# Attention with a gated MLP on one core: transposes two tiles behind the scores and the values' products three

## Chip, core and metric

The kernel runs on one core of a Trainium2 chip. The metric is the device time of one execution in microseconds. A core has five engines that run side by side, each through its own queue in order: PE (TensorE, matmuls and transposes), DVE (VectorE), ACT (ScalarE), POOL (GpSimd) and SP, whose queue issues all DMAs of this kernel.

## What is computed

Banded causal attention with sinks for 4 batches of 8 heads, 768 positions and 64 columns a head; then, on its output, an MLP with a convolution of three taps in its gate.

```python
scores = q @ k.T / sqrt(64)                    # per batch and head
keep = (key < n_sink) | ((row - key >= 0) & (row - key < window))
a = softmax(where(keep, scores, -1e9))
x = concat_heads(a @ v)                        # 4 x 768 x 512
h = maximum(x @ w_in, 0)                       # 4 x 768 x 1024
c = cw[0]*prev_row(h) + cw[1]*h + cw[2]*next_row(h)
out = (h * sigmoid(c)) @ w_out                 # 4 x 768 x 512
```

n_sink is 4 and the window 128. The weights and the taps arrive as 64-bit numbers, everything else in 32 bits.

## The kernel before

**Tiles.** Heads go in pairs: four pairs a batch, 16 pairs in all, g = 0 to 15. A pair has six tiles of 128 rows, t = 0 to 5, in two halves of three. A tile needs the scores of its own 128 keys, of the 128 before, and of the sinks. `jobs` lists the (pair, half); batch 0 takes all first halves of its four pairs, then all second halves, later batches both halves of a pair in turn. `steps` has one entry for each of the 96 tiles.

**One tile** has three parts. `scores(g, t)` makes the scores of both heads in two PSUM buffers (sc). In batch 0 the mask is a matmul of PE (L521, before the product L337), DVE takes the row minimum (L523) and ACT the exponential (L532); later two products (L340, L341) are masked on DVE (L528, L529). DVE adds and inverts the sums (L534, L535), POOL normalises (L537). `transp(g, t)` transposes the normalised tile (pe, in batch 0 in roomH and roomL) on PE into pts (L553 in batch 0, L567 later), ACT copies it to pT (L555, L569), and POOL cuts it to the band (L571, L573). After a half's third tile the sinks' part is transposed too (L560, L581). `pv(g, t)` works at a half's third tile only: the products with the values (px: L598, L606; sinks' part L609), then xH and xL, the high and low part of x (L348, L349).

**The MLP** runs in units of 256 rows and 128 of the 1024 columns, 96 units: twelve products ph (L185), a gate on ACT, DVE and POOL (L192 to L203, of which L197, L198 and L200 are DVE's), and six products po (L212) two units later. A unit needs x of its rows, so the first eight start after batch 0's first halves, and each batch's units run beside the next batch's attention; those of the last batch run alone at the end.

**Weights.** Sixteen blocks of 128 x 512 and the taps are loaded, narrowed from 64 bits and split into a high and a low part by ACT (L113), DVE (L114, L115, L116, the cast L123) and POOL (L124), one block a step from step 2 to 18 (`WHEN`).

**Keys, queries, values.** `prep` transposes keys (trk, tk) and queries (trq, tq) ahead of their pair. From pair 4 on the keys stand in a tile kk whose halves are swapped by two DMAs (L301, L302). Two buffers serve kk; in batch 0 they are kks[0] and kks[1], and kks[1] also holds the sinks' values that L609 of batch 0 reads. `values(n)` loads the values of job n into one of two tiles vraw, by two DMAs; the tile was read by the products of job n - 2.

**What sets the order.** The loop hands out, in step i, the scores of step i in slot 0, the transposes of step i - D1 in slot 1 and the products of step i - D2 in slot 2, with pieces of MLP and of `prep` after each slot:

```python
for slot in range(SLOTS):
    if slot == 0 and i < NST:
        scores(g, t)
    if slot == 1 and 0 <= i - D1 < NST:
        transp(*steps[i - D1][1:])
    if slot == 2 and 0 <= i - D2 < NST:
        pv(*steps[i - D2][1:])
```

This order is a rank, not yet the order of an engine's queue: the program is built with `schedule_with_timeline_sim=True`, and in the compiled rows work stands ahead of work of a lower step where that was ready sooner. The functions that the diff touches:

Of the kernel before, what the change touches and what calls it, by code (L numbers as in the profile page):

```python
# [365 lines left out]
def load_v(c, g, slot, lo=0, hi=None):  # L366
    hi = hi or c.S // P
    load(c, g, "v", c.v_raw[slot][:, lo:hi], lo, hi)
    return c.v_raw[slot]
# [12 lines left out]
def sink_split(c, m, vsr, b):  # L382

    raw, hi, lo = (m.mp.tile([P, 512], d, tag="st", name=f"sink{n}{b}", bufs=3)[0:NS] for d, n in ((F32, "r"), (F32R, "h"), (F32R, "l")))
    c.nc.sync.dma_start(raw.rearrange("s (h d) -> s h d", d=D), c.v[b].rearrange("h s d -> s h d")[0:NS])
    c.nc.scalar.copy(hi, raw)
    c.nc.vector.tensor_tensor(out=lo, in0=raw, in1=f(hi), op=ALU.subtract)
    for u in range(3):
        for part, val in enumerate((hi, hi, lo)):
            for j in range(2):  # L390
                r = SR * part + 2 * NS * u + NS * j
                dst, src = (f(x).rearrange("s (g j d) -> s g j d", j=2, d=D)[:, :, j] for x in (vsr[r:r + NS, u], val))
                c.nc.sync.dma_start(dst, src)


def banded(c):
# [5 lines left out]
    NPAIR = c.H // 2  # L402
# [35 lines left out]
    def masks():  # L438
        nc.vector.tensor_scalar(before, R, 0.0, None, ALU.is_lt)
        nc.vector.tensor_tensor(out=m0, in0=own, in1=sk, op=ALU.max)  # L440
        nc.vector.tensor_copy(m1[:, 0:NS], tmp[:, 0:NS])
        nc.vector.tensor_copy(m2[:, 0:NS], sk[:, 0:NS])
        for mk in (m1, m2):
            nc.vector.tensor_tensor(out=mk[:, NS:KW], in0=own, in1=prv, op=ALU.max)
        for mk in (m0, m1, m2):
            nc.vector.tensor_scalar(mk, mk, -NEG, NEG, ALU.mult, ALU.add)
# [9 lines left out]
    def clear():  # L456
        w = vsr.shape[1] * vsr.shape[2] // 2
        for h in range(2):
            nc.sync.dma_start(f(vsr).rearrange("p u n -> p (u n)")[:, w * h:w * h + w], A.zeros[0:3 * SR, 0:w])
# [15 lines left out]
    jobs = [(g, half) for half in range(2) for g in range(NPAIR)]  # L475
# [13 lines left out]
    def fetch(upto=len(queue)):  # L489

        while free[0] and asked[0] < min(len(queue), upto):
            free[0] -= 1
            g, nm, half = queue[asked[0]]
            st[g].raw[nm, half] = load_half(c, g, nm, half, c.raw[asked[0] % RAWB])
            asked[0] += 1
# [89 lines left out]
    def pv(g, t):  # L585

        s = st[g]
        hp = g % NPAIR
        hf, u = divmod(t, 3)
        if u < 2:  # L590
            return
        px = ps.tile([P, 3, P], F32, tag="px", name=f"px{g}_{hf}").rearrange("p t k -> p (t k)")
        first = 3 * hf
        tiles = range(first + 2, max(0, first - 1) - 1, -1)
        if g < NPAIR:
            for n, (t1, w) in enumerate((t1, w) for t1 in range(t, first - 1, -1) for w in range(1 + (t1 > 0))):
                for j in range(2):
                    nc.tensor.matmul(px[D * j:D * j + D, P * (t1 - first):P * (t1 - first) + P], s.v[:, t1 - w, j, :],  # L598
                                     s.pT[t1][:, w, j, :], start=(n == 0), stop=False, skip_group_check=True)
            tiles = ()  # L600
        for kt in tiles:
            pT = s.pT.pop((kt, hf)).rearrange("p h a k -> p h (a k)")
            lo, hi = max(kt, first), min(kt + 1, first + 2)
            cols = slice(P * (lo - kt), P * (hi - kt) + P)
            for j in range(2):
                nc.tensor.matmul(px[D * j:D * j + D, P * (lo - first):P * (hi - first) + P], s.v[:, kt, j, :], pT[:, j, cols],  # L606
                                 start=(kt == tiles[0]), stop=False, skip_group_check=True)
        for w in range(1 - hf, 3):
            nc.tensor.matmul(px[:, P * w:P * w + P], (vsr if g >= NPAIR else c.vs)[:, w, P * hp:P * hp + P], s.sT, start=False, stop=(w == 2),  # L609
                             skip_group_check=True)  # L610
        A.xout(g, hf, px)

    def prep(n):

        g, half = jobs[n]
        if g >= NPAIR and half:
            return []
        if g >= PLAIN:
            return A.prep(g, st[g], ahead)
        out = []  # L620
        for h in (half, half + 1)[0:1 + g // NPAIR]:
            out += A.prep32(g, h, st[g], kks[g // 2][:, g % 2], "po" if g < NPAIR and h == 0 else "h", ahead)
        return out

    def values(n):
        g, half = jobs[n]
        if g < NPAIR:
            st[g].v = load_v(c, g, n % 2, *((2, T) if half else (0, 3)))
        elif half == 0:
            st[g].v = load_v(c, g, g % 2)  # L630

    def coming(n):

        last = 2 * NPAIR - 2
        if n < last:
            return [(n + 1, -0.4, 1.8)]
        if n == last:
            return [(n + 1, -0.4, 1.4), (n + 2, 1.4, 5.6)]
        return [(n + 2, -0.4 if n > last + 2 else 1.8, 5.1)] if n % 2 == 0 and n + 2 < len(jobs) else []
# [8 lines left out]
    steps = [(n, g, 3 * half + u) for n, (g, half) in enumerate(jobs) for u in range(3)]  # L648
    NST = len(steps)
    NSTB = NPAIR * T  # L650
    D1, D2 = 1, 2
    SLOTS = 3
    fill, todo, after = [], [], None
    rate = acc = 0.0
# [4 lines left out]
    for i in range(NST + D2):  # L659
        if i < NST:  # L660
            n, g, t = steps[i]
            if t % 3 == 0:
                for n1, lo, hi in coming(n):
                    new = prep(n1)
                    todo += [(i + lo + (hi - lo) * (k + 1) / len(new), x) for k, x in enumerate(new)]
            if g >= NPAIR or t % 3 == 2:
                fetch()
            if t == 0 and g and g % NPAIR == 0:
                after = i + 3 if g > NPAIR else i
            if i == after:  # L670
                sink_split(c, m, vsr, g // NPAIR)
            if n + 1 < len(jobs) and (t % 3 == 2 if n < 2 * NPAIR else t == 3):
                values(n + 1)
        if i == NSTB // 2:
            clear()
        if i == NSTB - 3:
            masks()
        m.need(min(sum(i >= w for w in WHEN), len(m.todo)))
# [7 lines that stand above are left out]
                if i - D2 + 1 in cuts:  # L686
                    while fill:
                        fill.pop(0)()
                    lo, hi, span = cuts[i - D2 + 1]
                    fill = m.pieces(lo, hi)  # L690
                    rate = len(fill) / (span - 0.5)
                    acc = 0.0
            acc += rate / SLOTS
            while acc >= 1.0 and fill:
                fill.pop(0)()
                acc -= 1.0
            while todo and i + (slot + 1) / SLOTS >= todo[0][0]:
                todo.pop(0)[1]()
# [73 lines left out]
def attention_gated_mlp(ctx: ExitStack, tc: tile.TileContext, q, k, v, n_sink, window, w_in, conv_w, w_out, out):  # L772
# [33 lines left out]
    with tc.If(fast == 1) as cmp:  # L806
        with ExitStack() as es:
            c.es = es
            banded(c)
# [32 lines left out]
```

## Time and profile before

| | us |
|---|---|
| three runs | 500.57, 503.0, 502.32; median 502.32 |
| the profiled execution | 501.29 |
| its span, first to last instruction | 499.6 |
| PE busy | 465.2 (93%) |
| DVE busy | 350.5 (70%) |
| ACT busy | 342.2 (69%) |
| POOL busy | 311.1 (62%) |

Busy times are sums over the whole span, which has stages with different limits. PE's busy time includes matmuls that overlap the one before, so a full PE shows 100% with spacing shorter than its rows' lengths. The views that matter are the busy time by stretch, the waits by engine, and single rows of the timeline (start, length, engine, line, operation, tile written <- tiles read).

### The profile page before, as it was taken

The page shows a single profiled execution, that of the slowest core. Times are in us where ns is not written, and L with a number is a line of the kernel's source. Part 1 is how long each engine was busy: PE and PEld are TensorE (multiplying, and loading weights), DVE is VectorE, ACT ScalarE, POOL GpSimd, SP SyncE. Part 2 cuts the span into 40 slices and gives each one's busy share as a digit, 9 for nine tenths or more (in the row PEclk, how much of TensorE's full clock was granted, in tenths as well). Part 3 has the DMA queues.
Part 4 walks back from the last instruction along what each step waited for, and adds up shares of the span by engine and source line. Part 5 has one row for each costly group of instructions (what it writes and reads, how often), then busy time and mean ns, then how long its engine had stood idle before and what let it go on. Part 6 is the DMA issues. An engine that isn't in the chain of part 4 may idle for free.

```text
span 499.6 us, 10664 instructions
## 1 busy us (share of the span) xinstructions
PE 465.2 (93%) x3301; PEld 398.3 (80%) x3301; DVE 350.5 (70%) x1140; ACT 342.2 (69%) x1072; POOL 311.1 (62%) x582
## 2 busy tenths in 40 slices
PE   1786889999999999999999999999999999999993
PEld 1564666888788788888888889898888888899982
DVE  5799999466778777877667687776676665655561
ACT  3877675777878877887776787786776754545541
POOL 3458768456759596786767767684764564444341
PEclk9999889999999999999999999999999999999999
DMA  6786833444341524415142231424021100101001
GB/s 156 202 232 176 216 94 87 93 110 113 108 113 33 141 47 97 94 27 141 47 107 52 61 109 33 100 61 98 2 75 33 43 2 0 45 1 43 22 23 50
DMA packets 87307, 41.04 MB, mean 82 GB/s; under 512 B 80160, under 2 KB 80184, under 8 KB 87240
## 3 DMA queue, kind: packets, MB, share of 16 engines
q1 hardware_dynamic: 87240, 40.25, 31.1%
q8 instruction: 29, 0.48, 0.4%
q14 instruction: 38, 0.31, 0.2%
HBM read 27.60 MB, written 6.29 MB: 68 GB/s over the span
## 4 chain that ended last, share of the span: by engine, by line
PE 77%; DVE 10%; ACT 4%; POOL 3%; DMA 2%; issue 2%; SPq 0%; POOLq 0%; DVEq 0%; ACTq 0%
PE ph L185 26%; PE po L212 25%; PE px L606 6%; PE sc L340 3%; PE sc L341 3%; PE pts L567 3%; PE tq L273 2%; PE px L609 2%; PE sc L337 2%; DVE stm L115 2%; PE px L598 1%; DVE stm L116 1%; PE tk L291 1%; POOL roomH L537 1%; PE pts L553 1%
## 5 line engine op out<-in xcount | busy, mean ns | idle before, releaser
L212 PE MATMUL po<-woH,g 128*128 128x512 f32 x384 | 142.9, 408 | 1.5 <-POOL g L202 1.5
L185 PE MATMUL ph<-xH,wiH 128*128 128x258 f32 (+1 forms) x384 | 112.2, 292 | 0.0
L185 PE MATMUL ph<-xH,wiL 128*128 128x258 f32 (+1 forms) x384 | 109.2, 284 | 0.0
L185 PE MATMUL ph<-xL,wiH 128*128 128x258 f32 (+1 forms) x384 | 109.1, 285 | 0.0
L202 POOL TENSOR_SCALAR g<-t 128x256 fp32r<-128x256 f32 x96 | 42.0, 438 | 68.6 <-DVE t L200 48.4
L197 DVE SCALAR_TENSOR_TENSOR t<-hb,cw,t 128x256 f32<-128x256 f32 x96 | 56.7, 591 | 32.8 <-ACT t L196 32.3
L212 PEld LDWEIGHTS po<-woH,g 128*128 128x128 f32 x384 | 69.3, 189 | 12.3 <-POOL g L202 2.5
L203 POOL TENSOR_TENSOR g<-t,g 128x256 fp32r<-128x256 f32 x96 | 75.2, 783 | 5.6
L537 POOL TENSOR_SCALAR pe<-pe,sm 128x132 f32<-128x132 f32 (+1 forms) x144 | 60.3, 430 | 27.8 <-DVE sm L535 18.8
L185 PEld LDWEIGHTS ph<-xH,wiH 128*128 128x128 f32 x384 | 73.0, 190 | 4.4 <-issue 1.3
L212 PE MATMUL po<-woL,g 128*128 128x512 f32 x192 | 76.4, 398 | 0.0
L185 PEld LDWEIGHTS ph<-xH,wiL 128*128 128x128 f32 x384 | 73.0, 190 | 2.2
L185 PEld LDWEIGHTS ph<-xL,wiH 128*128 128x128 f32 x384 | 72.9, 190 | 0.8
L532 ACT ACTIVATE pe<-pe,sm 128x132 f32<-128x132 f32 (+1 forms) x144 | 58.0, 406 | 14.0 <-DVE sm L529 13.1
L199 ACT ACTIVATE t<-t 128x256 f32<-128x256 f32 x96 | 40.2, 418 | 34.9 <-DVE t L198 34.4
L200 DVE SCALAR_TENSOR_TENSOR t<-t,hb 128x256 f32<-128x256 f32 x96 | 46.9, 489 | 18.0 <-ACT t L199 17.6
L198 DVE SCALAR_TENSOR_TENSOR t<-hb,cw,t 128x256 f32<-128x256 f32 x96 | 54.2, 564 | 4.5
L192 ACT ACTIVATE hb<-ph 128x258 f32<-128x258 f32 (+1 forms) x96 | 37.0, 386 | 27.5 <-PE ph L185 26.9
L196 ACT ACTIVATE t<-hb,cw 128x256 f32<-128x256 f32 x96 | 49.3, 514 | 7.3 <-POOL g L203 3.2
L528 DVE COPY_PREDICATED sc<-before,sc 128x128 f32<-128x128 int32 x120 | 33.6, 291 | 19.0 <-PE sc L341 17.7
L571 POOL TENSOR_SCALAR_AFFINE_SELECT pT<-pT 128x256 f32<-128x256 f32 x60 | 27.1, 451 | 31.1 <-ACT pT L569 28.3
L529 DVE CUSTOM_DVE_ANT_0 pe<-sc,m 128x132 f32<-128x132 f32 (+1 forms) x144 | 39.8, 289 | 8.6 <-PE sc L341 7.2
(147 smaller groups left out, 1030.3 us busy)
## 6 DMA issues: line engine op xcount, KB each, us to landing
raw<-in_q_dram SPq DMA_DIRECT2D x64, 96.0 KB
raw<-in_k_dram SPq DMA_DIRECT2D x64, 96.0 KB
out_dram<-stm SPq DMA_DIRECT2D x24, 256.0 KB
kk<-kk SPq DMA_DIRECT2D x24, 198.0 KB
vraw<-in_v_dram SPq DMA_DIRECT2D x24, 192.0 KB
wi_0r<-in_moe_w_in_dram SPq DMA_DIRECT2D x2, 512.0 KB
wi_1r<-in_moe_w_in_dram SPq DMA_DIRECT2D x2, 512.0 KB
wi_2r<-in_moe_w_in_dram SPq DMA_DIRECT2D x2, 512.0 KB
```

What stands on the lines that cost most here:

```text
L185: nc.tensor.matmul(u.h[:, 0:W], w[:, cc, ff * P:(ff + 1) * P], x[:, cc, t0:t1], start=(i == 0), stop=(i == len(prods) - 1))
L196: nc.scalar.mul(a, prev, cw[:, 0, ff:ff + 1])
L197: nc.vector.scalar_tensor_tensor(out=e, in0=this, scalar=cw[:, 1, ff:ff + 1], in1=a, op0=ALU.mult, op1=ALU.add)
L198: nc.vector.scalar_tensor_tensor(out=a, in0=nxt, scalar=cw[:, 2, ff:ff + 1], in1=e, op0=ALU.mult, op1=ALU.add)
L199: nc.scalar.activation(e, a, AF.Tanh)
L200: nc.vector.scalar_tensor_tensor(out=a, in0=e, scalar=1.0, in1=this, op0=ALU.add, op1=ALU.mult)
L202: nc.gpsimd.tensor_scalar(u.g[:, 0], a, 1.0, 1.0, ALU.mult, ALU.mult)
L203: nc.gpsimd.tensor_tensor(out=u.g[:, 1], in0=a, in1=f(u.g[:, 0]), op=ALU.subtract)
L212: nc.tensor.matmul(po[:, 0:c.DM], u.g[:, a, tt * P:(tt + 1) * P], w[:, ff, :], start=(ff == 0 and i == 0), stop=(ff == NFF - 1 and i == 2))
L529: nc.vector.tensor_tensor_reduce(out=pe[:, j, cols], in0=pc[:, P:SW][:, cols], in1=mk, op0=ALU.add, op1=ALU.min, scale=1.0, scalar=3.0e38, ...
L532: nc.scalar.activation(pe[:, j, cols], pcs[j][:, cols] if alone else pe[:, j, cols], AF.Exp, bias=sm[:, j:j + 1], scale=-1.0, accum_out=sm ...
L537: nc.gpsimd.tensor_scalar(pe[:, j, cols], pe[:, j, cols], sm[:, 8 + j:9 + j], 1.0, ALU.mult, ALU.mult)
```

## The change

D1 and D2 grow by one: a step hands out the transposes of the tile two steps back and the products of the tile three steps back; the loop runs one pass longer at its end, and the MLP's pieces, which are cut when a product is handed out, come one step later. The load of the next job's values moves from the head of the step, before its scores, to slot 2, behind that step's products.

```diff
-    D1, D2 = 1, 2
+    D1, D2 = 2, 3
     SLOTS = 3
...
             if i == after:
                 sink_split(c, m, vsr, g // NPAIR)
-            if n + 1 < len(jobs) and (t % 3 == 2 if n < 2 * NPAIR else t == 3):
-                values(n + 1)
...
                     rate = len(fill) / (span - 0.5)
                     acc = 0.0
+            if slot == 2 and i < NST and n + 1 < len(jobs) and (t % 3 == 2 if n < 2 * NPAIR else t == 3):
+                values(n + 1)
             acc += rate / SLOTS
```

Three places of the compiled order follow. In the names, sc_3_1 is a score buffer of tile 3, head 1; the last number is a running number.

First place: DVE at the cast of the last weight block (wo7r), in batch 0's second halves. Before:

```order
L523 TENSOR_REDUCE sm_170<-sc_5_1_997 128x1
L200 SCALAR_TENSOR_TENSOR t_943<-t_944,hb_114 128x256
L116 SCALAR_TENSOR_TENSOR stm_1029<-stm_1030,stm_1029 128x512
L523 TENSOR_REDUCE sm_171<-sc_3_0_1037 128x1
L534 TENSOR_REDUCE sm_170<-sm_170 128x2
L123 CAST woH<-stm_1029 128x512
L197 SCALAR_TENSOR_TENSOR t_1057<-hb_115,cw,t_1056 128x256
```

And now, with the same last cast of woH:

```order
L523 TENSOR_REDUCE sm_170<-sc_5_1_948 128x1
L197 SCALAR_TENSOR_TENSOR t_977<-hb_114,cw,t_976 128x256
L116 SCALAR_TENSOR_TENSOR stm_1010<-stm_1011,stm_1010 128x512
L349 TENSOR_TENSOR xL_117<-px_1_986,xH_116 128x384
L198 SCALAR_TENSOR_TENSOR t_976<-hb_114,cw,t_977 128x256
L534 TENSOR_REDUCE sm_170<-sm_170 128x2
L123 CAST woH<-stm_1010 128x512
L535 RECIPROCAL sm_170<-sm_170 128x2
L523 TENSOR_REDUCE sm_171<-sc_3_0_1018 128x1
L200 SCALAR_TENSOR_TENSOR t_976<-t_977,hb_114 128x256
```

The third unit's gate (L197, L198, L200) has moved later against the weights, its last row from before the cast to after it, and so has the next tile's first minimum (sc_3_0).

Second place: PE at the second score of the fourth tile of pair 2, which stands near that cast. Before:

```order
L212 MATMUL po_971<-woH,g_889 128x512
L212 MATMUL po_1010<-woH,g_889 128x512
L212 MATMUL po_1010<-woL,g_889 128x512
L212 MATMUL po_1010<-woH,g_889 128x512
L553 MATMUL pts<-ident,roomL 128x128 x4
L521 LDWEIGHTS identb
L521 MATMUL sc_3_1_1038<-apart_145,identb 128x260
L337 MATMUL sc_3_1_1038<-kks_165,X_901 128x260
L212 MATMUL po_971<-woH,g_950 128x512
```

And now:

```order
L315 MATMUL trq_1047<-ident,raw_69 128x128 x3
L185 MATMUL ph_1042<-xH_116,wiL 128x258
L185 MATMUL ph_1042<-xL_117,wiH 128x258
L185 MATMUL ph_1042<-xH_116,wiH 128x258
L185 MATMUL ph_1042<-xH_116,wiL 128x258
L553 MATMUL pts<-ident,roomL 128x128 x2
L521 LDWEIGHTS identb
L521 MATMUL sc_3_1_1019<-apart_145,identb 128x260
L337 MATMUL sc_3_1_1019<-kks_165,X_865 128x260
L553 MATMUL pts<-ident,roomL 128x128 x2
L185 MATMUL ph_1042<-xL_117,wiH 128x258
L212 MATMUL po_1006<-woH,g_920 128x512
```

The po products of the second unit (g_889 before, g_920 now) stood ahead of the score and now stand behind it; two of the four transposes too.

Third place: PE ahead of the first score of pair 5 (sc_0_0), which reads the second tile kk. Before:

```order
L185 MATMUL ph_1633<-xH_116,wiL 128x260
L185 MATMUL ph_1633<-xL_117,wiH 128x260
L609 MATMUL px_0_1717<-sT_0_1631,vsr 128x128 x2
L273 MATMUL tq_1642<-identr,nq_1638 128x128 x3
L567 MATMUL pts<-ident,pe_1_1600 128x128 x2
L273 MATMUL tq_1651<-identr,nq_1638 128x128 x3
L273 MATMUL tq_1712<-identr,nq_1708 128x128 x3
L340 MATMUL sc_0_0_1789<-kk_1569,X_1641 128x128
```

And now:

```order
L341 MATMUL sc_5_1_1686<-kk_1133,X_1308 128x260
L567 MATMUL pts<-ident,pe_1_1570 128x128 x2
L606 MATMUL px_0_1740<-pT_2_0_1654,vraw_71 64x128 x2
L606 MATMUL px_0_1740<-pT_1_0_1593,vraw_71 64x256 x2
L606 MATMUL px_0_1740<-pT_0_0_1519,vraw_71 64x256 x2
L273 MATMUL tq_1616<-identr,nq_1612 128x128 x3
L273 MATMUL tq_1626<-identr,nq_1612 128x128 x3
L567 MATMUL pts<-ident,pe_1_1570 128x128
L581 MATMUL tk_2_1658<-identr,sk_0_1659 72x128
L340 MATMUL sc_0_0_1760<-kk_1521,X_1615 128x128
```

The twelve ph of a unit, which stood between the products px of pair 4 and this score, have moved behind it. Counted back from this score to the transposes of the second half of the pair's keys (tk), there stood 12 ph and 9 tq among others; now there are one ph and 6 tq, beside the same px.

## Prediction before the run

> **What bounds the kernel now.** I read the stretches first, one row per stage: length, then busy time (and instructions) of PE, of PE's weight loads, of DVE, ACT and POOL, then clock, DMA share and GB/s.
>
> ```profile
> 12.00:25.00 13.00, 10.31 (x57) 7.92 (x58) 9.34 (x32) 10.62 (x36) 6.11 (x11) 1.00 0.77 207
> 25.00:84.00 59.00, 48.95 (x349) 37.87 (x348) 56.62 (x127) 41.11 (x121) 42.21 (x46) 0.94 0.62 170
> 84.00:100.00 16.00, 14.97 (x109) 11.76 (x108) 8.88 (x23) 11.66 (x34) 9.70 (x15) 1.00 0.33 74
> 100.00:200.00 100.00, 97.62 (x745) 84.02 (x743) 74.08 (x287) 78.84 (x272) 69.81 (x140) 1.00 0.39 95
> 200.00:425.00 225.00, 225.00 (x1632) 195.91 (x1631) 158.30 (x580) 162.79 (x532) 149.97 (x300) 1.00 0.24 60
> 425.00:499.60 74.60, 66.59 (x413) 59.31 (x411) 37.12 (x69) 33.09 (x77) 29.36 (x48) 0.99 0.09 31
> ```
>
> Two regimes. From 25 to 84 us VectorE is busy 56.62 of 59 us: it narrows and splits the weights beside the softmax, and only 2.4 us are left in it. From 84 us TensorE is the bound (225.00 of 225 between 200 and 425); the last 66 us are MLP alone. So a wait of PE counts only after 84 us, and a rearrangement before that counts only if it saves DVE time or leaves less PE work for later. PE's waits after 84 us, from the view of waits (total, times, longest):
>
> ```profile
> PE po L212 <- POOL g L202: 1.5, 2, 1.2
> PE pts L553 <- POOL roomL L537: 0.8, 1, 0.8
> PE sc L340 <- DVE sm L529: 0.7, 2, 0.5
> PE px L606 <- POOL pT L573: 0.5, 2, 0.3
> PE pts L567 <- POOL pe L537: 0.3, 1, 0.3
> PE sc L521 <- ACT roomH L532: 0.3, 1, 0.3
> PE tq L273 <- DVE kk L297: 0.2, 1, 0.2
> PE sc L521 <- ACT roomL L532: 0.2, 1, 0.2
> ```
>
> They sum to 4.5 us. The 1.2 of the first row is the last unit's gate near the end, which nothing here touches; 3.3 us remain. That is all a longer distance between a tile's scores and its transposes can win in the part where PE sets the time. Before 84 us PE waits much more, but under a busy DVE.
>
> **The change, part by part.** No instruction is added or removed; each loop step hands out the same scores with transposes and products of one step earlier. The rows of the compiled order show how little of that reaches the engines: the three places shown with the change differ by a fraction of a tile, since the order takes work when it is ready and the loop gives only its rank. Prices for PE work come from the chain of waits, in which saturated PE work has its true spacing (start, length, what):
>
> ```profile
> 367.11 1.46 PE ph L185 x12
> 369.04 0.33 PE tk L291 x3
> 370.95 0.12 PE sc L341
> 372.76 1.40 PE po L212 x6
> 374.16 0.22 PE pts L567 x2
> 374.70 1.23 PE px L606 x12
> 105.58 0.20 PE tq L273 x3
> ```
>
> (a) *DVE up to the last weight* (first place). The cast of the last weight block closes the DVE-bound stretch:
>
> ```profile
> 82.02 0.41 DVE L200 SCALAR_TENSOR_TENSOR t<-t,hb 128x256 f32<-128x256 f32 x1
> 82.95 0.42 DVE L523 TENSOR_REDUCE sm<-sc 128x1 f32<-128x260 f32 x1
> 83.35 0.41 DVE L123 CAST woH<-stm 128x512 fp32r<-128x512 f32 x1
> ```
>
> Counted from the first weight cast to this row, the order holds 148 DVE rows before and 146 now: the same weight work, 18 tiles' sums, five xL, three units' L197 and L198; one L523 and one L200 now come after it. That is 0.42 + 0.41 = **-0.8 us**.
>
> (b) *PE work left over.* At that cast PE stands, in both orders, near the second score of the fourth tile of pair 2 (82.75 us in the trace, the second place). Ahead of it stood 48 L185 and 12 L212; now 47 and 6. Six L212 cost 1.40, one L185 0.12. Two transposes of pe fewer (0.22 by the pts row) and three of q more (0.33, taken from the tk row) give back 0.1. So PE enters its saturated part with **+1.4 us** more to do: the lag delays the MLP's first products. Its bounds are 0 (PE, which had waits there, catches up) and one whole unit, 1.46 + 1.40 = 2.9.
>
> ```profile
> 82.75 0.27 PE L521 MATMUL sc<-apart,identb 128*128 128x260 bf16 x1
> ```
>
> (c) *Waits after 84 us.* Of the 3.3 us, none would go at worst and all at best. In the order the way from a tile's scores to its transposes, and between two scores in one buffer, has grown at more places than it has shrunk, though by far less than a tile. I take half, **-1.6 us**.
>
> (d) *The keys of pair 5.* Their tile is a buffer of batch 0, in which the sinks' values lie until the last L609 of that batch; the second half of the keys is transposed (tk), cast, and swapped between partition halves by two DMAs (L301, L302) before the pair's first score may run.
>
> ```profile
> 124.20 0.49 PE L291 MATMUL tk<-ident,raw 128*128 128x128 f32 x3
> 126.62 0.53 SPq L302 DMA_DIRECT2D kk<-kk  x1
> 130.63 0.30 PE L340 MATMUL sc<-kk,X 128*128 128x128 f32 x1
> 128.00:129.00 1.00, 1.00 (x11) 1.00 (x10) 0.96 (x6) 0.46 (x3) 0.54 (x2) 1.00 0.80 234
> 129.00:129.70 0.70, 0.69 (x7) 0.50 (x6) 0.51 (x2) 0.70 (x3) 0.70 (x2) 1.00 0.05 18
> ```
>
> The DMA share falls from 0.80 to 0.05 near 129 us, so tk to landing is about 4.8 us and tk to score was 6.4. The order now puts less PE work between them (third place): 3 tk (0.33), 1 ph (0.12), 4 score products (0.48), 3 pts (0.33), 12 px (1.23), 6 tq (0.40) and the sinks' transpose (0.1, one third of a tk row), 2.95 us together, against 4.8 before (11 ph more, the values' sinks, 3 tq, a pts). PE must then idle 4.8 - 2.95 = 1.9 us there; it idled 6.4 - 4.8 = 1.6 before. Were the keys slower by the whole 1.6 us of that slack, it would be 1.9 more; were they at once ready, 1.6 less. I take **+0.5**. Behind the waiting score on PE stands the MLP, and all of it is late by that much. On ACT the cast of the first half of these keys now stands ahead of the last xH of batch 0; both wait for the same L609, so xH is one cast later on an engine that is busy 78.84 of 100 us: 0.
>
> (e) *The loads of v* move from the head of a step to behind that step's product, and wait for the job before last, one step later. SP issues two of 0.97 us together; behind them in its queue now stands the load of wi_2r, which was ahead:
>
> ```profile
> 46.90 0.42 SPq L102 DMA_DIRECT2D wi_2r<-in_moe_w_in_dram  x1
> 47.38 0.97 SPq L357 DMA_DIRECT2D vraw<-in_v_dram  x2
> 57.82 0.85 DVE L115 SCALAR_TENSOR_TENSOR stm<-wi_2r,stm 128x512 int32<-128x512 int32 x1
> 18.79 4.39 DMA wi_2r<-in_moe_w_in_dram
> ```
>
> Such a block took 4.39 us to land when the chain waited for its twin, so there are 57.82 - 46.90 - 4.39 = 6.5 us of cover for a delay of one or two: **0**. If the cover were gone, DVE would wait in the stretch that it bounds, microsecond for microsecond. The v tiles themselves are read six steps later in batch 0 and eight later on: 0.
>
> (f) *The end.* One more pass of the loop; the last batch's MLP pieces still follow the last product on a full PE: 0.
>
> Sum: -0.8 + 1.4 - 1.6 + 0.5 + 0 = **-0.5 us** on an execution that took 501.29 us (span 499.6 and 1.7 around it), so 500.8. The three runs have their median 1.0 us higher, at 502.32 (500.57 to 503.0); on that footing **501.8 us**. About 0.5%, 2.5 us, is what a measurement of this kernel can tell from no change. My forecast is within it; by itself it has +-2 us, from the bounds of (b), (c) and (d).
>
> **Rivals.** *Faster:* the lag does what its name says, and every wait on a tile's chain goes: all 3.3 us after 84, DVE's 2.4 us of idle between 25 and 84, and no new wait at pair 5. 501.3 - 0.8 + 1.4 - 3.3 - 2.4 = 496.2, on the runs' footing **497.2 us**. For it: PE's waits for normalised tiles between 12 and 84 us, 5.5 us in two rows. Against it: DVE is busy 96% of the stretch from 25 to 84, and the order hardly moves. Chance 0.20.
>
> ```profile
> PE pts L553 <- POOL roomH L537: 3.5, 4, 1.5
> PE pts L553 <- POOL roomL L537: 2.0, 2, 1.7
> ```
>
> *Slower, by DVE and POOL in each other's way.* The same DVE instruction takes two very different times in the stretch that DVE bounds:
>
> ```profile
> 35.35 0.68 DVE L116 SCALAR_TENSOR_TENSOR stm<-stm,stm 128x512 int32<-128x512 int32 x1
> 46.17 1.62 DVE L116 SCALAR_TENSOR_TENSOR stm<-stm,stm 128x512 int32<-128x512 int32 x1
> L116 DVE SCALAR_TENSOR_TENSOR stm<-stm,stm 128x512 int32<-128x512 int32 (+1 forms) x15 | 13.7, 910 | 0.1
> ```
>
> The mean of 910 ns over 15 against 0.68 is 3.5 us, about four long ones at 0.94 us extra each. The order of weight work against softmax has changed, and POOL's normalisations and low halves fall beside other DVE rows. Four more long ones are +3.8: 501.8 + 3.8 = **505.6 us**; from three more it is slower than can be taken for noise. For it: nothing in the order avoids it; against it: as many could vanish. Chance 0.14.
>
> The Trainium skill, "SBUF — State Buffer", section "Who interferes with whom", has a rule for such pairs: a DVE instruction with two SBUF inputs and a GpSimd one that reads SBUF use one port pair under an exclusive lock, and the later one is blocked fully. The trace agrees so far as one and the same instruction takes 0.68 us at one place and 1.62 at another. By that rule which of the two starts first decides, which only the new trace shows; the sum could come out 3.5 us lower or higher by it, 498.3 to 505.3, and without it stays at 501.8.
>
> *The keys of pair 5 are late as a whole:* if the way from the last L609 of batch 0 to the first score of pair 5 (119.3 + 0.8 to 130.6, 10.5 us) has to be walked again, with 6.7 us of PE work in it now against 9.0 before (by the prices above: 18 ph, 3 tk, 3 tq, a pts and two of the sinks' products fewer, three po more), PE idles 3.8 instead of 1.5: +2.3 for +0.5, **503.6 us**. It decides when the work there is shorter than the way. Chance 0.08.
>
> ```profile
> 119.28 0.83 PE L609 MATMUL px<-sT,kks 96*128 96x128 f32 x6
> ```
>
> *The change does not do what it says,* since order follows readiness, is inside the forecast (502.3), whose chance is 0.58.
>
> **How the numbers follow.** The likeliest case gives 501.8. A little over half of the fast rival lies below 498.0 (0.11) and half of the port rival above 505.6 (0.07); that leaves out 0.18, so the range is 498.0 to 505.6. Faster by over 0.5%: the fast rival and 0.02 of the forecast's edge, 0.22. Slower: 0.14 and 0.04, 0.18. Within: 0.60.
>
> **What would show it.** In the new profile: (a) the last woH cast near 83 us, DVE near 56 of 59 us before it; (b) twelve instead of eighteen L212 before the first score of the next tile; (c) the pts and sc rows of PE's waits after 84 us halved, the rest the same; (d) a wait of a microsecond or two ahead of the first L340 of pair 5; (e) no wait of DVE or ACT on a weight load that was not there before. A cast later than 86 us, with L115 and L116 longer, means the port rival; a PE wait of over 2 us at pair 5 the keys; a cast before 81 us the fast one. What would make it all wrong is a wait that the order cannot show, in a queue that I priced at nothing.

## Result and profile after the change

| | before | after |
|---|---|---|
| median of the runs side by side, us | 501.77 (4 runs) | 508.99 (4 runs) |
| ratio, 95% interval | | 1.0143 (1.0113 to 1.0173) |
| the profiled execution, us | 501.29 | 508.26 |
| its span, us | 499.6 | 506.3 |

The kernel became 1.4% slower, 3.4 us above the upper end of the predicted range. The stretches of the changed kernel, with the columns of the prediction's first view:

```profile
12.00:25.00 13.00, 10.20 (x54) 7.55 (x55) 9.01 (x31) 10.23 (x34) 6.01 (x10) 1.00 0.76 201
25.00:84.00 59.00, 48.23 (x348) 37.45 (x349) 55.89 (x122) 39.86 (x116) 41.84 (x45) 0.94 0.61 171
84.00:100.00 16.00, 13.48 (x86) 10.89 (x86) 10.09 (x27) 12.26 (x36) 11.18 (x16) 0.89 0.35 78
100.00:200.00 100.00, 98.38 (x748) 84.71 (x748) 70.09 (x282) 78.38 (x265) 65.86 (x136) 1.00 0.38 93
200.00:425.00 225.00, 225.00 (x1600) 193.51 (x1599) 157.14 (x581) 163.20 (x535) 151.63 (x301) 1.00 0.24 61
425.00:506.30 81.30, 73.82 (x466) 65.39 (x464) 40.89 (x76) 36.07 (x83) 32.53 (x51) 0.99 0.08 28
```

The telling row is the fifth, and in it not the busy time but the count. PE is busy 225.00 of 225 us in both kernels, at the same clock, and does 1600 matmuls instead of 1632. At 225 / 1632 = 0.138 us each the missing 32 are 4.4 us. The other loss is ahead of 200 us: 24 matmuls fewer (1236 for 1260), 3.3 us by the same price, 23 of them between 84 and 100. A few records can be missing, so these are sizes, not accounts; they sum to 7.7 where the profiled executions differ by 7.0. Between 84 and 100 us the granted clock was also lower, 0.89 against 1.00, which these counts include.

PE's waits after 84 us in the changed kernel (total, times, longest):

```profile
PE sc L521 <- ACT roomH L532: 2.5, 1, 2.5
PE po L212 <- POOL g L202: 1.2, 1, 1.2
PE sc L340 <- DMA kk<-kk: 0.7, 1, 0.7
PE pts L567 <- POOL pe L537: 0.5, 1, 0.5
PE px L606 <- POOL pT L573: 0.2, 1, 0.2
PE ph L185 <- DVE kk L297: 0.2, 1, 0.2
```

Most of the small waits on a tile's chain went, as hoped for in (c). One of 2.5 us came. The timeline shows it on PE, and on ACT the queue ahead of the exponential that it waits for:

```profile
84.52 0.40 PE L212 MATMUL po<-woH,g 128*128 128x512 f32 x1
87.44 0.27 PE L521 MATMUL sc<-apart,identb 128*128 128x260 bf16 x1 [2.52 <-ACT roomH L532]
```

```profile
84.53 0.42 ACT L199 ACTIVATE t<-t 128x256 f32<-128x256 f32 x1 [2.37 <-DVE t L198]
85.38 0.62 ACT L386 CAST sinkh<-sinkr 4x512 fp32r<-4x512 f32 x1 [0.44 <-DMA sinkr<-in_v_dram]
85.91 1.03 ACT L252 ACTIVATE X<-trq,headscale 128x384 f32<-128x384 f32 x2
86.84 0.45 ACT L532 ACTIVATE roomH<-sc,sm 128x260 f32<-128x260 f32 x1
```

ACT stood idle for 2.37 us at a gate's step, then for 0.44 at the sinks' cast, with the exponential behind both.

The loss after 200 us is in no row of waits. It is seen where one half's products L606 stand in PE's order. Pair 9's second half in the compiled order of the changed kernel, with what stands between its pieces (running numbers left out):

```
L606 MATMUL px9_1<-pT9_5_1,vraw 64x128 x2
L291 MATMUL tk110<-ident,raw 128x128 x3
L606 MATMUL px9_1<-pT9_4_1,vraw 64x256 x2
L606 MATMUL px9_1<-pT9_3_1,vraw 64x256
L212 MATMUL po320<-woH,g32 128x512
L212 MATMUL po320<-woL,g32 128x512
L606 MATMUL px9_1<-pT9_3_1,vraw 64x256
L606 MATMUL px9_1<-pT9_2_1,vraw 64x128
L212 MATMUL po320<-woH,g32 128x512
...
L606 MATMUL px9_1<-pT9_2_1,vraw 64x128
```

Each operand pT serves two products, one for each head of the pair; a product fills 64 of the array's columns (128*64 in the trace), and is two matmuls there. This half is broken three times, twice between the two heads of a pair. From batch 1 on there are 24 halves; their products stood in 29 pieces before (5 breaks, 4 inside a pair of heads) and stand in 40 now (16 breaks, 11 inside). The changed kernel's timeline at this half, PE and then its weight loads:

```profile
258.04 0.44 PE L606 MATMUL px<-pT,vraw 128*64 128x128 f32 x4
258.41 0.55 PE L291 MATMUL tk<-ident,raw 128*128 128x128 f32 x3
258.88 1.08 PE L606 MATMUL px<-pT,vraw 128*64 128x256 f32 x6
259.89 0.50 PE L212 MATMUL po<-woH,g 128*128 128x512 f32 x1
260.23 0.39 PE L212 MATMUL po<-woL,g 128*128 128x512 f32 x1
260.55 0.65 PE L606 MATMUL px<-pT,vraw 128*64 128x256 f32 x4
261.12 0.73 PE L212 MATMUL po<-woH,g 128*128 128x512 f32 x2
...
262.25 0.43 PE L606 MATMUL px<-pT,vraw 128*64 128x128 f32 x2
262.61 0.39 PE L340 MATMUL sc<-kk,X 128*128 128x260 f32 x1
```

```profile
258.41 0.31 PEld L291 LDWEIGHTS tk<-ident,raw 128*128 128x128 f32 x3 [0.17 <-ACT t L199]
258.88 0.62 PEld L606 LDWEIGHTS px<-pT,vraw 128*64 128x64 f32 x6 [0.17 <-issue]
259.89 0.19 PEld L212 LDWEIGHTS po<-woH,g 128*128 128x128 f32 x1 [0.38 <-POOL g L202]
...
260.55 0.20 PEld L606 LDWEIGHTS px<-pT,vraw 128*64 128x64 f32 x4 [0.36 <-issue]
261.12 0.30 PEld L212 LDWEIGHTS po<-woH,g 128*128 128x128 f32 x2 [0.38 <-issue]
...
262.25 0.19 PEld L606 LDWEIGHTS px<-pT,vraw 128*64 128x64 f32 x2 [0.36 <-issue]
262.61 0.19 PEld L340 LDWEIGHTS sc<-kk,X 128*128 128x128 f32 x1 [0.17 <-issue]
```

From the start of a piece to the start of what follows it: 0.37 + 1.01 + 0.57 + 0.36 = 2.31 us for sixteen matmuls. At seven of the eight crossings between these and full-array matmuls the weight load, which otherwise runs beside the matmul ahead, stands still: for 0.36 to 0.38 us where work of 256 or 512 columns stood ahead, for 0.17 us behind work of 128 columns alone. At the first crossing (258.04) no idle time is listed.

### The profile page after: what moved, and what is told of

The parts are those of the page before. It is cut to its first block, busy times and chain, and to the rows that moved or that the text cites. A ratio compares the mean times of both kernels' runs of the same rounds, so it can differ in the third digit from the quotient of the medians.

```text
span 506.3 us, 10673 instructions
## 1 busy us (share of the span) xinstructions
PE 470.9 (93%) x3301; PEld 401.1 (79%) x3301; DVE 349.3 (69%) x1140; ACT 344.1 (68%) x1072; POOL 313.0 (62%) x582
## 4 chain that ended last, share of the span: by engine, by line
PE 82%; DVE 9%; DMA 3%; ACT 2%; issue 1%; POOL 1%; SPq 0%; POOLq 0%; ACTq 0%; DVEq 0%
PE ph L185 27%; PE po L212 26%; PE px L606 7%; PE sc L340 4%; PE sc L341 3%; PE pts L567 3%; PE tq L273 2%; DVE stm L115 2%; DVE stm L116 2%; PE px L609 2%; PE sc L337 2%; PE tk L291 2%; PE px L598 2%; PE pts L553 1%; DVE sm L523 1%
## 5 line engine op out<-in xcount | busy, mean ns | idle before, releaser
L197 DVE SCALAR_TENSOR_TENSOR t<-hb,cw,t 128x256 f32<-128x256 f32 x96 | 56.9, 592 | 34.9 <-ACT t L196 34.0
L537 POOL TENSOR_SCALAR pe<-pe,sm 128x132 f32<-128x132 f32 (+1 forms) x144 | 62.6, 447 | 25.8 <-DVE sm L535 18.4
L199 ACT ACTIVATE t<-t 128x256 f32<-128x256 f32 x96 | 40.1, 418 | 38.9 <-DVE t L198 38.4
L200 DVE SCALAR_TENSOR_TENSOR t<-t,hb 128x256 f32<-128x256 f32 x96 | 46.5, 485 | 17.4 <-ACT t L199 16.7
L198 DVE SCALAR_TENSOR_TENSOR t<-hb,cw,t 128x256 f32<-128x256 f32 x96 | 53.0, 552 | 5.3 <-DVE t L197 0.5
L340 PE MATMUL sc<-kk,X 128*128 128x260 f32 (+1 forms) x144 | 44.5, 316 | 0.8 <-DMA kk<-kk 0.7
```

The lines of the kernel that those rows point to most:

```text
L197: nc.vector.scalar_tensor_tensor(out=e, in0=this, scalar=cw[:, 1, ff:ff + 1], in1=a, op0=ALU.mult, op1=ALU.add)
L198: nc.vector.scalar_tensor_tensor(out=a, in0=nxt, scalar=cw[:, 2, ff:ff + 1], in1=e, op0=ALU.mult, op1=ALU.add)
L199: nc.scalar.activation(e, a, AF.Tanh)
L200: nc.vector.scalar_tensor_tensor(out=a, in0=e, scalar=1.0, in1=this, op0=ALU.add, op1=ALU.mult)
L340: self.nc.tensor.matmul(pc, X[:, j, u, :], kk[:, j, lo:hi], start=True, stop=False)
L537: nc.gpsimd.tensor_scalar(pe[:, j, cols], pe[:, j, cols], sm[:, 8 + j:9 + j], 1.0, ALU.mult, ALU.mult)
```

## The experiments

Two of these kernels (e7, e8) only set D1 and D2 and the place of the load of v. In the others PE, DVE, ACT, POOL and SP keep a compiled order, with the named instructions moved by hand. For that a function at the end of the kernel ties each instruction to the one ahead of it on its engine, by edges that order but do not wait:

```python
for a, b in zip(names, names[1:]):      # one row of names for each engine
    c.tc.add_manual_dep(made[b], a, info, reason="order")   # info: NoSync
```

Holding an order in this way costs nothing that shows: e2, which holds the changed kernel's order with two instructions moved, took 508.96 us, the changed kernel 508.99. In e1 to e4 two lines of imports push all line numbers up by two (L608 there is L606). All were timed in five rounds beside the kernel before; ratios are to it.

### Mending the breaks: e1 and e4

Edit, on PE alone; here at the half shown above (e4 the same on the kernel before):

```diff
-L606 MATMUL px9_1<-pT9_5_1,vraw 64x128 x2
 L291 MATMUL tk110<-ident,raw 128x128 x3
-L606 MATMUL px9_1<-pT9_4_1,vraw 64x256 x2
-L606 MATMUL px9_1<-pT9_3_1,vraw 64x256
...
+L606 MATMUL px9_1<-pT9_5_1,vraw 64x128 x2
+L606 MATMUL px9_1<-pT9_4_1,vraw 64x256 x2
+L606 MATMUL px9_1<-pT9_3_1,vraw 64x256 x2
+L606 MATMUL px9_1<-pT9_2_1,vraw 64x128 x2
```

> The changed kernel, its order held on every engine by order-only edges, with one thing moved: on PE the products L606 of one half, which stand in 40 pieces for 24 halves (29 before the change), stand in 24, each half where its last piece was; nothing is left out. Theory A, that PE pays about 0.3 us for each break of such a group (in the trace 0.20 us from L606 to what follows and 0.09 us back): 16 breaks fewer, 508.3 - 4.6 = 503.7 us. Theory B, that the loss is the wait of 2.5 us at 84 us and the half clock behind it, and that the slow growth after 180 us is something else: 508.3 us. Theory C, that pieces fill holes in which PE would wait: slower, by up to the 16 holes of 0.1 to 0.3 us, 510 to 513 us.

> The kernel before the change, order held, the products L606 of a half kept together: 24 pieces instead of 29. Theory A: 5 breaks by 0.29 us, 501.3 - 1.5 = 499.8 us. Theory B: 501.3 us. Theory C: 501.8 to 503 us.

Measured: e1 502.00 us, 1.0006 (0.9992 to 1.0020), 7.0 us less than the change; e4 498.63 us, 0.9935 (0.9916 to 0.9954), 2.7 us less than its session's 501.28. Theory A holds in sign; its price of 0.29 us a break was too low: 7.0 / 16 = 0.44 and 2.7 / 5 = 0.53. The same stretch as above, in e1 and in e4, and a whole half of sixteen matmuls in e1:

```profile
200.00:425.00 225.00, 224.13 (x1645) 197.47 (x1645) 160.03 (x583) 163.67 (x536) 154.60 (x303) 1.00 0.24 60
```

```profile
200.00:425.00 225.00, 225.00 (x1653) 197.88 (x1652) 158.77 (x583) 165.02 (x538) 151.92 (x304) 1.00 0.24 61
```

```profile
312.11 1.52 PE L608 MATMUL px<-pT,vraw 128*64 128x128 f32 x16
313.56 0.39 PE L342 MATMUL sc<-kk,X 128*128 128x260 f32 x1
```

In this stretch e1 does 45 matmuls more than the changed kernel, and e4 does 21 more than the kernel before. Whole, a half takes 1.45 us where it took 2.31 in four pieces.

### Breaking them on purpose: e5 and e6

Edit, on PE, in each of e4's 24 halves: the instruction ahead of the half goes behind its second pair (e5) or behind the first product of the second pair (e6):

```diff
-L567 MATMUL pts<-ident,pe10_0 128x128
 L606 MATMUL px9_1<-pT9_5_1,vraw 64x128 x2
 L606 MATMUL px9_1<-pT9_4_1,vraw 64x256 x2
+L567 MATMUL pts<-ident,pe10_0 128x128
 L606 MATMUL px9_1<-pT9_3_1,vraw 64x256 x2
```

> The kernel of e4 (before the change, the products L606 of a half kept together), with each of the 24 halves broken once, behind its second pair of heads: the one PE instruction that stood ahead of the half stands in the break. Nothing is left out. In the trace the two heads' products of 256 columns start 7 ns apart and the next pair 0.21 us later, and a half costs 0.10 us more where it goes over to another line and 0.09 us where it is come back to. By that a break between pairs costs 0.2 us: 498.6 + 24 x 0.2 = 503.4 us. If every break costs the same, whatever it parts (0.41 us, the 6.6 us of e1 by 16): 508.5 us. If breaks are not the cause, and e1 and e4 are faster for another reason that comes with the order: 498.6 us.

> As e5, but each half broken once inside a pair, behind the first head's product of the second pair. If the price is that the two heads' products no longer run side by side: 0.2 us as in e5, and 0.21 us for the product that now runs alone, 498.6 + 24 x 0.41 = 508.4 us. If every break costs the same: the same as e5. If breaks are not the cause: 498.6 us.

Measured: e5 508.25 us, 1.0130 (1.0108 to 1.0151); e6 516.74 us, 1.0298 (1.0274 to 1.0322). Against e4 that is 9.6 / 24 = **0.40 us** for a break between pairs and 18.1 / 24 = **0.75 us** inside one. Both prices are about twice the expected ones, and they differ, so it is not any break alike. The timeline of PE at one and the same half of six products (pairs of 128, 256 and 256 columns), with a query's transpose L273 in the break, in e5 and then in e6:

```profile
304.51 0.87 PE L606 MATMUL px<-pT,vraw 128*64 128x128 f32 x8
305.31 0.28 PE L273 MATMUL tq<-identr,nq 128*128 128x128 f32 x1
305.52 0.65 PE L606 MATMUL px<-pT,vraw 128*64 128x256 f32 x4
306.11 0.44 PE L273 MATMUL tq<-identr,nq 128*128 128x128 f32 x3
```

```profile
307.52 0.86 PE L606 MATMUL px<-pT,vraw 128*64 128x128 f32 x6
308.32 0.28 PE L273 MATMUL tq<-identr,nq 128*128 128x128 f32 x1
308.53 1.08 PE L606 MATMUL px<-pT,vraw 128*64 128x256 f32 x6
309.54 0.28 PE L273 MATMUL tq<-identr,nq 128*128 128x128 f32 x1
```

From start to next start, the first piece takes 0.80 us in both, though in e6 one of its products has gone; the second piece takes 0.59 us in e5 and 1.01 with that product in it. So a lone product takes the time of a pair. When they are not parted, the second head's product runs beside the first in the other 64 columns: 1.01 - 0.59 = 0.42 us is the price of parting them, 0.35 by the runs (0.75 - 0.40). My expectation had counted a product as one matmul, where the trace has two, and so at half its price.

### One lag at a time: e7 to e10

Edit of e7: `D1, D2 = 2, 2`, the load of v at its old place. Edit of e8: `D1, D2 = 1, 3`, the load moved as in the change. e9 and e10 are e7 and e8 with their breaks mended as in e1. (There is no run with the load of v moved alone. With D1 and D2 as before, that move leaves the compiled order of PE, DVE, ACT and POOL as it was; in SP's queue one load of v falls behind two stores of the output.)

> The transposes trail by two tiles, the products by two as before, the loads of v at their old place; the order is what comes of it. On PE the products L606 have 18 breaks, 11 of them inside a pair (before 5 and 4, after 16 and 11). Counting 0.2 us for a break and 0.21 more inside a pair, 5.9 us against 1.8 before: 501.3 + 4.1 = 505.4 us, and up to 2.5 us more if the losses ahead of 150 us come with the transposes: 507.9 us. If the longer lag of the products is the cause: 501.3 us.

> The products trail by three tiles, with the loads of v moved as in the change, the transposes by one as before. On PE the products L606 have 14 breaks, 8 of them inside a pair: by the same count 4.5 us against 1.8 before, 501.3 + 2.7 = 504.0 us, and up to 2.5 us more if the losses ahead of 150 us come with the products: 506.5 us. If the transposes' lag is the cause: 501.3 us.

> The kernel of e7 (only the transposes trail by two), order held, its 18 breaks of the products L606 mended on PE; nothing is left out. If the breaks are the whole of its loss, at the 0.44 us (e1) to 0.53 us (e4) that a mended break gave: 507.5 - 18 x 0.44 to 0.53 = 498.0 to 499.6 us, level with e4. If the longer lag of the transposes costs something by itself, the rest of it stays: above 500.5 us.

> The kernel of e8 (only the products trail by three), order held, its 14 breaks mended. By the same price: 502.1 - 14 x 0.44 to 0.53 = 494.7 to 495.9 us. By its own trace, in which PE's progress falls behind that of the kernel before by only 2.1 us after 180 us, so that its breaks are cheap ones: 502.1 - 2.1 - 2.9 (what e4 gained there) = 497.1 us. If a longer lag of the products gains nothing and e8's trace misleads: 498.6 us, level with e4.

| transposes, products trail by | as compiled | breaks (inside a pair) | breaks mended |
|---|---|---|---|
| 1, 2 (before) | 501.77 | 5 (4) | e4 498.63, 0.9935 (0.9916 to 0.9954) |
| 2, 2 | e7 507.53, 1.0121 (1.0099 to 1.0144) | 18 (11) | e9 497.80, 0.9934 (0.9910 to 0.9957) |
| 1, 3 | e8 502.06, 1.0012 (0.9997 to 1.0026) | 14 (8) | e10 495.68, 0.9885 (0.9866 to 0.9904) |
| 2, 3 (the change) | 508.99, 1.0143 (1.0113 to 1.0173) | 16 (11) | e1 502.00, 1.0006 (0.9992 to 1.0020) |

e7, e9 and e10 came within 0.2 us of their expectations; e8 came 1.9 us below the 504.0 counted from its breaks. At 0.40 and 0.75 us the breaks in the four rows should be worth 3.4, 11.1, 8.4 and 10.3 us; mending gave 2.7 to 3.1, 9.7, 6.4 and 7.0, some 70 to 90%. (Not all are between products of 256 columns, as in e5 and e6.) So the breaks make all of what e7 loses, and about half of what the change loses. With them mended, trailing products gain 0.5% over e4: e10 is the fastest version, 6 us below the kernel before, and why the lag gains there was not looked into. e9, with trailing transposes, is level with e4; but the products of batch 0 (L598), which no run mended, stand in 8 pieces there, one for each half, and in 12 in e4, so that a small cost of the lag may be hidden. Both lags together cost 3.4 us (502.00 against 498.63) that neither costs alone, and 6.3 us against e10.

### The loss ahead of 115 us: e2, e3 and e11 to e15

Edits, each of instructions moved in their engine's queue between 84 and 107 us, on the changed kernel (e2) or on e1 (the others):

```diff
+e2, e3  DVE: L523 sm<-sc2_3_0 ahead of L349;  ACT: L532 roomH<-sc2_3_0 ahead of L199
+e11      DVE: L534, L535 ahead of L349;  POOL: L537 x2 ahead of the last L124
+e12      ACT: L555 pT1_4<-pts ahead of L199
+e13      ACT: L264 nq40, L264 nq50 behind L192 hb<-ph4
+e15      PE: L185 ph5 x12 ahead of L521 sc3_4_0
```

e3 is e2 with the breaks mended; e11, e12, e13 and e15 each add a line to the one before; e14 is e1 with the line of e13 alone.

> The changed kernel, order held, with two instructions moved near 84 us: on DVE the row minimum L523 of the first score of tile 3 of pair 2 stands ahead of L349, on ACT its exponential L532 stands ahead of the gate's L199, the sinks' cast L386 and the two copies L252. Nothing is left out. If PE's wait of 2.5 us there is the place of that exponential in ACT's queue: the wait goes, and PE, which the clock then need not slow, ends 2.2 to 3 us earlier, 505.3 to 506.1 us. If the rest of PE has slack for it, or the wait moves to the next score: 508.3 us.

> The two together. If the loss consists of these two alone and they add: 508.3 - 4.6 - 2.5 = 501.2 us, the time of the kernel before. If one of them hides the other: no better than the better of the two, 503.7 us or 505.7 us.

> The kernel of e3 with the wait that took the place of the one removed taken away too: near 85 us, DVE's sum and reciprocal L534 and L535 of tile 5 of pair 1 also stand ahead of L349, and on POOL the two scalings L537 of that tile stand ahead of the subtraction L124 of the last piece of weights. Nothing is left out. If the changed kernel's loss ahead of 150 us comes from the order of those queues: the wait of 2.4 us at the transposes L553 goes, 502.5 - 2.4 = 500.1 us, down to e4's 498.6 us if the clock stays up. If each such wait only hands its slack on to the next, or the last piece of weights is then late for the units: 502.5 us.

> The kernel of e11 with one more instruction moved: on ACT the copy L555 of the transposes of tile 4 of pair 1, for which the next transposes wait (in e11 it ended at 87.18 us and they began at 87.33), stands right behind the exponential, ahead of L199, the sinks' cast L386 and the copies L252, which wait for DVE and for a DMA. Nothing is left out. If ACT's queue is what holds PE at 84 to 88 us: PE's wait of 2.2 us there goes, and the time comes to 501.3 - 2.2 = 499.1 us, near e4's 498.6. If PE's time there is slack that later waits (1.2 us for the gate at 102 us, 0.8 us for the keys of pair 5) take back: 501.3 us.

> The kernel of e12 with the two casts L264 of q (pairs 4 and 5), for whose loads ACT stands still for 2.8 us until 95.27 us, moved on ACT behind the work that is ready there: two exponentials L532, the key casts L294 and L299, the copies L555 and L348 and the gate's L192. Nothing is left out. If that queue is what costs the changed kernel its 3.4 us: PE's waits of 0.6 us at the score and 1.2 us for the gate at 100 to 103 us go, 502.0 - 1.8 to 3.4 = 498.6 to 500.2 us. If the loss is neither there: 501.3 to 502.0 us. If the casts are then late for the first queries of batch 1: a new wait at L273, over 502 us.

> The kernel of e1 (products together, nothing else moved) with the same two casts L264 moved. If the wait for the load is the loss and the waits at 84 to 88 us are slack: as e13. If both have to go before either shows: as e1, 502.0 us, while e13 is faster. If neither counts: both 502.0 us.

> The kernel of e13 with the twelve products L185 of the next unit (104.69 to 106.22 us there) moved on PE ahead of the score L521 at which it waits 1.5 us. Nothing is left out. If PE's idle time ahead of 115 us is what remains of the change's loss, and comes from its fixed order: 12 x 0.12 = 1.4 us of the wait are filled, 500.9 - 1.4 = 499.5 us. If the work is only missing later, at the next score: 500.9 us.

| | us | ratio, 95% interval |
|---|---|---|
| e2 | 508.96 | 1.0143 (1.0121 to 1.0165) |
| e3 | 502.53 | 1.0014 (1.0000 to 1.0029) |
| e11 | 501.30 | 0.9997 (0.9980 to 1.0013) |
| e12 | 502.03 | 1.0006 (0.9991 to 1.0020) |
| e13 | 500.87 | 0.9987 (0.9971 to 1.0004) |
| e14 | 503.83 | 1.0049 (1.0030 to 1.0067) |
| e15 | 504.54 | 1.0043 (1.0030 to 1.0056) |

The wait of 2.5 us goes in e2, and the time stays. PE's wait near 87 us in e2, and its wait in e11:

```profile
87.53 1.36 PE L555 MATMUL pts<-ident,roomL 128*128 128x128 f32 x4 [2.43 <-POOL roomL L539]
```

```profile
87.33 0.63 PE L553 MATMUL pts<-ident,roomL 128*128 128x128 f32 x4 [2.21 <-POOL g L202]
```

In e2 the exponential was in time, and the transposes behind it waited for POOL. In e11 POOL's scalings had ended at 85.39 us, and the row names POOL only because it came last by the profile: ACT's copy L555 of the transposes before, still behind L199 and L386, ended at 87.18. e12 moved that copy, and the wait near 87 us broke into 0.26 and 1.26 us, with no gain. In e13 and e15 PE stood at these rows:

```profile
101.50 0.27 PE L521 MATMUL sc<-apart,identb 128*128 128x260 bf16 x1 [1.50 <-ACT roomL L532]
102.83 0.49 PE L212 MATMUL po<-woH,g 128*128 128x512 f32 x1 [0.62 <-POOL g L202]
```

```profile
103.80 0.58 PE L185 MATMUL ph<-xH,wiH 128*128 128x258 f32 x1 [3.42 <-ACT X L252]
```

e13 and e14 took away another standstill of ACT, 2.7 us at the cast L264 behind a load of q: 500.87 us with the earlier moves; without them 503.83, slower than e1's 502.00, which no case of its expectation had. So it is not the owner either. e15 is a plain miss: the products that I took for ready need a PSUM buffer that the queries' transposes hold until ACT has copied them (L252), and PE stood there 3.42 us instead of 1.50.

So of the 3.4 us no single wait is the owner: four versions (e3, e11, e12, e13), in which the longest waits were taken away one after the other, took 500.9 to 502.5 us, and with e1 they cannot be told apart well. How far PE has come by 115 us, in e1 and in e4:

```profile
0.00:115.00 115.00, 88.45 (x607) 70.30 (x608) 89.29 (x226) 76.08 (x223) 68.43 (x107) 0.96 0.57 150
```

```profile
0.00:115.00 115.00, 91.08 (x632) 72.10 (x633) 90.44 (x238) 78.71 (x233) 70.35 (x110) 0.96 0.56 149
```

e1 is 25 matmuls behind, 3.5 us by the price above, at the same clock; e11, e12 and e13 stand at 607 as well, so what they won at one wait was lost again by then. (The distance is 12 matmuls by 200 us and 18 by 425; as matmuls differ in length, the place is likely and not proven.) One rival was not run. The products of batch 0 (L598) stand in 12 pieces before and in e4, and in 14 in the changed kernel, in e1 and in all runs of this section: 4 and 6 breaks, 4 and 5 inside a pair. By the prices of e5 and e6 that is 0.40 + 0.75 = 1.2 us of the 3.4; and e10, which has the 14 pieces too, has no such loss. **What makes both lags together cost 3.4 us stays open.** That it is the order of the in-order queues ahead of 115 us, one wait standing behind the next, is argued from these rows and not shown, since no run removed the loss.

## Why the prediction was wrong

**The step that failed** is the sentence that prices PE's work "in which saturated PE work has its true spacing", with twelve px for 1.23 us. It took a matmul to cost the same wherever it stands, so in the stretch in which PE is full nothing could change unless work was moved out of it, and the compiled order was read at three places only. But the price of L606 hangs on its neighbours. The order held the answer without a run: 40 pieces against 29. At the measured prices the 11 more breaks (7 of them inside a pair) are 4 x 0.40 + 7 x 0.75 = 6.9 us; mending was worth 7.0 - 2.7 = 4.3 us more here than in the kernel before, of the 7.7 us between 508.99 and that session's 501.28, and by the ratios 3.6 of 7.2 us: about half. It decided the miss: an estimate without it, 508.99 - 4.3 = 504.7 us, lies inside the range. The other half is the 3.4 us that e1 still loses against e4, where the terms (a) to (c) sum to -1.0; which of them fails for it stays open. No rival contained the price of breaks. The last sentence looked for the surprise in "a wait that the order cannot show"; it was a cost that the order shows and the list of waits can't, since a PE that pays it counts as busy.

The Trainium skill, "TensorEngine Tiling (Array Packing)", section "Key Properties", says that a change of tiling mode drains TensorE. The trace agrees as far as the weight load stands still, for 0.17 to 0.38 us, at seven of the eight crossings between 128*64 and 128*128 in the half shown, and e5 puts 0.40 us on a break with its two crossings. The prediction should have weighed this rule.

(a) *DVE up to the last weight:* the sign was wrong. The cast came at 84.48, 1.1 us later than before instead of 0.8 earlier. From the first weight cast to this one, before and now:

```profile
14.19:83.35 69.16, 56.43 (x393) 43.12 (x390) 63.12 (x148) 50.32 (x150) 47.69 (x56) 0.95 0.66 179
14.19:84.48 70.29, 56.71 (x394) 43.28 (x392) 63.19 (x146) 49.28 (x147) 47.85 (x55) 0.95 0.63 176
```

The two rows fewer were there, but the other rows took as much longer, so DVE is busy just as long; and it stands idle for 7.10 us instead of 6.04, a change that the term put at nothing. Single long rows, of which the port rival spoke, are there, and were there before:

```profile
81.87 1.76 DVE L116 SCALAR_TENSOR_TENSOR stm<-stm,stm 128x512 int32<-128x512 int32 x1
...
84.48 0.41 DVE L123 CAST woH<-stm 128x512 fp32r<-128x512 f32 x1
```

A L115 of 1.77 us stood near the cast before (79.99 us). All rows together grew by 0.9 us, not by the 3.8 that the rival needed; its 505.6 us was nearer to the time for a reason that did not decide it.

(b) *PE work left over:* the sign was right. PE was busy 48.23 us there against 48.95, 0.7 less, half of the 1.4.

(c) *Waits after 84 us:* without the last unit's 1.2, 3.3 us became 4.1 instead of 1.7. All but 0.7 us of the old ones went, and the new waits of 2.5 and 0.7 us took their place. As to price, e2 and e12 show that taking this wait away gains nothing by itself.

(d) *Keys of pair 5:* the wait at L340 for the swapped keys is there, 0.7 us, and the listed waits of PE from the transposes of the keys to this score rose from 0.5 to 1.4 us, for the +0.5. The way to that number was wrong: PE did not idle 1.6 us there before, since its work took longer than its list of prices, and the sign asked for a wait of one or two microseconds. (The listed terms also sum to 2.99, not 2.95.) That the size is near is partly luck.

(e), (f) *Loads of v, the end:* right, nothing. ACT's waits for weight loads sum to 2.1 us for 2.2 before, DVE has none, and the last stretch does its work at about the same pace, 466 matmuls in 81.3 us against 413 in 74.6.

## What to carry to other kernels

Where an engine is full, compare how many instructions it completes in a stretch, not how busy it is. Before pricing a reordering, count in the compiled order how often groups of matmuls on part of the array are torn, and whether a pair that runs side by side is parted: here each tear cost 0.40 to 0.75 us (e5, e6), and keeping the groups whole was worth 2.7 us on the kernel before (e4), where the change was forecast to win 0.5. And where a scheduler turns a small change of rank into a new order, test the change with the order's accidents taken out: the trailing products looked neutral (e8) and are the better version (e10).

## What the runs showed of the hardware

That a product on 64 columns had no price of its own here: beside the other head's it took no time of its own (0.80 us for the piece with it and without it), alone it cost 0.42 us at 256 columns. And that a change between 64-column and full-array matmuls cost 0.40 us for going and coming back (e5), which the list of PE's waits does not show; in the half shown only the weight loads show it, with 0.17 to 0.38 us idle at most crossings.
